# A fused Mamba-2 scan and mixture of experts on one core: how the decays of chunks 2 to 5 are made

## The chip, the core and the metric

The kernel runs on one core of a Trainium2 chip. Five engines work side by side, each through its own list of instructions in order: TensorE (PE in the profile; PEld is its weight load) multiplies matrices, VectorE (DVE) and GpSimd (POOL) work element by element, ScalarE (ACT) copies and applies functions such as the exponential, and SyncE (SP) issues most of the transfers (ScalarE issues a few). An engine that must wait for another waits on a semaphore, and everything behind that instruction in its list waits with it. TensorE writes its results to eight banks of an accumulation memory; a bank is free again when whoever reads it is done.

The metric is the device time of one execution in microseconds. The kernel before took 614.96 us, the median of three runs (614.61 to 615.97).

## The reference

Two parts follow each other. The first is a state-space scan (4 sequences, 8 heads, 768 steps, head width 32, state width 16). The reference takes the steps in chunks of 32; the kernel takes chunks of 128, which gives the same result. The second is a mixture of 4 experts on the 3072 tokens that come out, 256 wide, with 1024 hidden features in each expert.

```python
la = log(clip(a, 1e-6, 1));  cum = cumsum(la)            # within a chunk
L  = exp(cum[i] - cum[j]) * (i >= j)                     # the decays
y  = (C B^T * L) x + (C state) * exp(cum[i])
state = exp(cum[last]) * state + sum_j B_j x_j exp(cum[last] - cum[j])
...
p   = domain_probs / sum(domain_probs)
out = sum over experts e of p[:, e] * (relu(y @ w1[e]) @ w2[e])
```

L, the lower triangle of products of `a` between step j and step i, is what this case is about: each chunk of 128 steps and each head needs a square of 128 by 128 such decays.

## The kernel before

There are 24 chunks of 128 tokens; chunk c belongs to sequence c % 4, so chunks 0 to 3 are the first of their sequences and have no earlier state. Chunks go in pairs (two chunks share a token tile of 256 columns), and three pairs make a block; the experts' products on a block are done while the scan of the next block is under way.

**The experts.** `product` (L933) is the bulk of TensorE's work: two matmuls in the program of 128 by 128 weights against 256 columns, each shown as two records in the profile. For the first pair, chunks 0 and 1, the plain form is used: `plain_first(fb)` for four blocks fb of 256 hidden features, then the second layer. Everything after that uses sums and differences of weights and of tokens (a fast matrix product), made by DVE and POOL (L1024 for weights, L1043 for tokens, L960, L968, L1071 and others for the intermediate results). L968 applies the ReLU and the gate.

**The scan.** For a pair, `score` (L502) multiplies C by B on TensorE, four banks for the four quarters of the heads. The score is multiplied by the decays on DVE (L856), and `inner` (L546) multiplies the result with x and gives the outputs and the new state; `outputs` calls it for both chunks of a pair. `fade` (L540, POOL) makes the columns that lead to the state. `mask` (L495) makes the masked C.

**Three ways to the decays.** Chunks 0, 1 and 2: rows of `a` are loaded, clipped and set to zero at the first step, spread by TensorE over all partitions (`spread`, L660, ones against the rows, into four banks), and multiplied up by a scan on DVE (`scan`, L519, four of 256 columns for each chunk), which leaves the triangle L in the tile LT0. Chunks 3, 4 and 5 (`c < SCANNED`, 6): a transfer spreads the clipped rows over all partitions (`load_decays`, L463, 512 KB each, from the copy `acut_d`), and DVE scans two stretches of 512 columns. Chunks 6 and on: ScalarE takes the logarithm of `a`, DVE sums it along a chunk (L725), the sums go to `cum_d`; a transfer spreads a chunk's sums over the partitions, ScalarE makes exp(cum[i] - cum[j]) with -cum[j] as bias (`decay`, L526, one for each head), and POOL cuts the upper triangle away (`causal`, L531).

**The order.** Up to the first product the list is written out by hand: warm-up matmuls (`idle`, L684), chunks 0 and 1, the gates. The gates of the first block: the probabilities come by ScalarE's first DMA (L570), POOL and DVE turn them into shares (L614 to L619, with DVE's reciprocal in L618), TensorE transposes them (L646) into `p_sb`, and spreads those of four chunks (`spread_gate`, L652). From there on a planner (`Plan`) orders the work: `line` fixes TensorE's order, each piece has a cost and a due time, and the other engines and SP take pieces by due time. The line of the first block before: spread of chunk 2, two product blocks, `bias` (L1360: transposes of the sums, for the exponentials' bias), scores of 2 and 3, two product blocks, a part of the second layer, outputs of 2 and 3, and so on with chunks 4 and 5.

Of the kernel before, what the change touches and what calls it, by code (L numbers as in the profile page):

```python
# [35 lines left out]
SCANNED = 6  # L36
SCORED, OWN, LEAD, LEFT = 5, 2, 5, 3
# [322 lines left out]
def kernel(  # L360
# [26 lines left out]
    SPREAD = 3  # L387
# [21 lines left out]
    acut_d = tc.dram_tile([NCH, NH, P], FP32, name="acut_d")  # L409
# [11 lines left out]
    def some(n, shape, name, pool=const):  # L421
# [19 lines left out]
        "dram": [None],  # L441
    }
# [18 lines left out]
    def load_decays(c, ab):  # L461
        src = acut_d if c < SCANNED else cum_d
        nc.sync.dma_start(  # L463
            out=ab, in_=src[real(c)].rearrange("h s -> (h s)").partition_broadcast(P))
# [28 lines left out]
    def mask(c, ctm, xb):  # L493
        for t in range(NT):
            nc.scalar.mul(ctm[:, t], xb[:, OCT:OCT + P], tmask[:, t:t + 1])  # L495
# [28 lines left out]
    def decay(c, MT, ab, neg, h):  # L524

        nc.scalar.activation(  # L526
            out=MT[:, place(c, h), 0:P], in_=ab[:, h * P:h * P + P], func=AF.Exp,
            bias=neg[:, h % NT, NQ * real(c) + h // NT:NQ * real(c) + h // NT + 1])

    def causal(MT, h, n):  # L530
        nc.gpsimd.affine_select(  # L531
            out=MT[:, h:h + n, 0:P], in_=MT[:, h:h + n, 0:P], compare_op=ALU.is_ge, fill=0.0,
            base=0, pattern=[[0, n], [1, P]], channel_multiplier=-1)

    def fade(c, MT, xb, LT):
        b = xb[:, OB:OB + HN].rearrange("p (h n) -> p h n", h=NH)
        n = NH // 2 if place(c, 0) else NH
        for h in range(0, NH, n):
            to = slice(place(c, h), place(c, h) + n)
            nc.gpsimd.tensor_mul(  # L540
                MT[:, to, P:], b[:, h:h + n], LT[:, to, P - 1:P].to_broadcast([P, n, N]))

# [8 lines left out]
    def keep_state(c, A, y):  # L551
# [8 lines left out]
    aq0 = homes["V"][-1][:, 0].rearrange("p (t s) -> p t s", t=NT)  # L560
    aq1 = homes["V"][-2].rearrange("p c (t s) -> p c t s", t=NT)
    a_q = [aq0, aq1[:, 0], aq1[:, 1]]
# [3 lines left out]
    a_sb = homes["cum"][0]  # L566
    a_cut = homes["V"][-4][:NCH * NH // 2, 0].rearrange("p (r s) -> p r s", r=2)
    nc.gpsimd.memset(aq0, 0.0)
    nc.vector.memset(aq1, 0.0)
    nc.scalar.dma_start(out=pr, in_=probs)  # L570
    a_rows = a.rearrange("(i k) (q t) s -> k q i (t s)", k=NC, t=NT)[0]
    nc.sync.dma_start(
        out=aq0.rearrange("(q r) t s -> q r (t s)", q=NQ)[:, 0], in_=a_rows[:, 0])
    nc.scalar.dma_start(
        out=aq1.rearrange("(q r) c t s -> q r c (t s)", q=NQ)[:, 0], in_=a_rows[:, 1:SPREAD])
    nc.scalar.preload_act_table_set("natural_log_exp_and_others")

    xb = homes["xb"]
    nc.sync.dma_start(out=xb[0][:, OBT:], in_=xbc[real(0)][:, OBT:])
    nc.sync.dma_start(  # L580
        out=a_sb, in_=a.rearrange("c h s -> (c h) s").rearrange("(p r) s -> p r s", r=2))
    nc.sync.dma_start(out=xb[1][:, OBT:], in_=xbc[real(1)][:, OBT:])
    for c in range(2):
        nc.sync.dma_start(out=xb[c][:, :OBT], in_=xbc[real(c)][:, :OBT])
    for fb in range(2):
        load_w1(fb, homes["W"][fb])
    load_tokens(2, xb[2])
# [5 lines left out]

    tmask = const.tile([P, NT], FP32)
    nc.vector.memset(tmask, 0.0)
    for q in range(NQ):
# [4 lines left out]
    nc.vector.memset(zeros, 0.0)  # L601
    own = const.tile([P, 1], FP32)
    nc.vector.reduce_sum(
        own.unsqueeze(2), ident[:, 0].rearrange("p (q r) -> p r q", r=32)[:, 0:1],
        axis=mybir.AxisListType.X)

# [3 lines left out]
    clip(nc.vector, aq0.rearrange("p t s -> p (t s)"), own)  # L610
    nc.vector.memset(aq0[:, :, 0:1], 0.0)
# [10 lines left out]
    clip(nc.vector, aq1.rearrange("p c t s -> p (c t s)"), own)  # L622
    nc.vector.memset(aq1[:, :, :, 0:1], 0.0)

    clip(nc.gpsimd, a_sb)
    nc.gpsimd.tensor_copy(a_cut, a_sb)
    nc.gpsimd.memset(a_cut[:, :, 0:1], 0.0)

    def store_decays(engine, d, sb):
        engine.dma_start(  # L630
            out=d.rearrange("c h s -> (c h) s").rearrange("(p r) s -> p r s", r=2), in_=sb)

    store_decays(nc.sync, acut_d, a_cut)
    load_tokens(3, xb[3])
    for fb in range(2, 4):
        load_w1(fb, homes["W"][fb])
    for fb in range(4):
        load_w2(fb, homes["W"][4 + fb])
    load_decays(3, homes["ab"][0])
# [9 lines left out]
    def spread_gate(bank, gate):  # L649
        g = bank.rearrange("p (c s) -> p c s", s=P)  # L650
        for c in range(4):
            nc.tensor.matmul(  # L652
                out=g[:, c], lhsT=ident[:rows, 0, c * E:c * E + 1].to_broadcast([rows, P]),
                rhs=p_sb, start=(c == 0), stop=True, skip_group_check=True)
        nc.scalar.copy(out=gate[:, :4], in_=g)

    def spread(c, banks):
        for q, b in enumerate(banks):
            k = slice(32 * q, 32 * q + 32)
            nc.tensor.matmul(  # L660
                out=b[:, :NT * P], lhsT=one[k].to_broadcast([32, P]),
                rhs=a_q[c][k].rearrange("p t s -> p (t s)"),
                start=True, stop=True, tile_position=(32 * q, 0))
# [44 lines left out]
    nc.scalar.activation(out=a_sb, in_=a_sb, func=AF.Ln)  # L708
    next_ = [BANK[4], BANK[0], BANK[1], BANK[6]]
    scan_quarters(1, LT[1], four, 0)  # L710
# [9 lines left out]
    spread_gate(BANK[5], homes["gate"][0])  # L720
    for r in (3, 1, 2):
        masked(1, r, MT[1], LT[1], next_[r], 0)
    sums = homes["cum"][1]
    for r in range(2):
        nc.vector.tensor_tensor_scan(  # L725
            out=sums[:, r], data0=a_sb[:, r], data1=zeros[:NCH * NH // 2], initial=0.0,
            op0=ALU.add, op1=ALU.add)
    store_decays(nc.sync, cum_d, sums)
    ys = []
    for t in range(NT):  # L730
        y = BANK[6 + t][:, :P + N]
        ys.append(y)
        inner(1, t, y, xb[1], MT[1], P + N, True)
        nc.scalar.copy(out=yT0[:, t, P:], in_=y[:, 0:P])
    for t, y in enumerate(ys):
        keep_state(1, A[1][:, t], y[:, P:])
    mask(2, ctm[0], xb[2])
    nc.sync.dma_start(out=p_d.rearrange("e c s -> c e s"), in_=p_sb)

# [5 lines left out]
    now = 13.2  # L745
# [24 lines left out]
    yT[0, 0] = plan.taken("V", NV - 3, now)  # L770
    aq = plan.taken("V", NV - 2, 0.0)
    plan.homes["V"][NV - 4].free = now + 3.0
    plan.homes["W"][NW - 1].free = now
    for c, i in ((2, 2), (3, 3)):
        st[c]["xb"] = plan.taken("xb", i, now)
    st[2]["ctm"] = plan.taken("ctm", 0, now)
    st[3]["ab"] = plan.taken("ab", 0, now + 2)
    for c in range(2):
        st[c]["A"] = plan.taken("A", c, now)
    g0 = gates[0, 0] = plan.taken("gate", 0, now)  # L780
    LTv = [plan.taken("V", i, now) for i in range(4)]
    cum, cd, neg = plan.taken("cum", 1, now), plan.taken("dram", 0, now + 3.0), value("neg")

    def fetch(c):
# [9 lines left out]
        if "ab" not in s and c >= SPREAD:  # L794
            s["ab"] = value("ab")
            dma(lambda e: load_decays(c, s["ab"].t), 1, 512, part=[s["ab"]],
                reads=[cd] if c >= SCANNED else [])

    def decays(c):
        s = st[c]  # L800
        j = c % 2
        if not j:
            s["MT"] = st[c + 1]["MT"] = value("MT")
            s["made"] = st[c + 1]["made"] = []
# [759 lines left out]
```

## Time and profile before

| What | Value |
|---|---|
| Median of three runs | 614.96 us (614.61 to 615.97) |
| The profiled execution | 617.03 us, its span 615.3 us |
| TensorE busy | 605.7 us, 98% of the span |
| DVE, ACT, POOL busy | 489.5, 292.5, 157.6 us |
| Moved by DMA | 99.65 MB, mean 162 GB/s |
| First product (L933) starts | 13.28 us |
| Scan of chunk 3 starts | 19.13 us |
| Outputs of chunks 2 and 3 | 24.98 to 27.19 us |

The span is the time from the first instruction to the last on the core; the execution's own time has 1.7 us more around it. Busy time of TensorE counts a matmul from its issue to a modelled end, so a slow or waiting stretch can hide in it: the waits and the granted clock say more. In the timeline each line has start, length, engine, source line, operation, output and input, shape, count, and in brackets the idle time before it with what ended it. Idle time of an engine that nobody waits for costs nothing.

### The profile page before, as it was taken

The numbers are of one execution on the slowest core, as the hardware profiler recorded it, in microseconds if no ns is written. First come the engines' busy times: TensorE is split into PE (matmuls) and PEld (weight loads), VectorE is DVE, ScalarE is ACT, GpSimd is POOL, SyncE is SP. The second block draws the span as 40 slices with busy tenths as digits, with TensorE's granted clock in tenths as the row PEclk, the third lists the DMA queues.
The fourth block names the chain that finished last, engine by engine and source line by source line (L and its number), as shares of the span: only waits on it lengthen the run. The fifth ranks groups of instructions, "written<-read, shape, count | busy, mean of one in ns | idle before, by whom it ended". The sixth has DMA issues, their size and how long they took to land.

```text
span 615.3 us, 10136 instructions
## 1 busy us (share of the span) xinstructions
PE 605.7 (98%) x3365; PEld 514.8 (84%) x3365; DVE 489.5 (80%) x854; ACT 292.5 (48%) x681; POOL 157.6 (26%) x238
## 2 busy tenths in 40 slices
PE   9899999999999999999999999999999999999997
PEld 5677878888888888888888888888888888888885
DVE  7879897998969895697978988386785979576775
ACT  4237646378651327877443333844444242434441
POOL 5536556636372000776500100210000000000000
PEclk9899999999999999999999999999999999999999
DMA  7737578676863429983442424964233232964001
GB/s 249 256 114 231 204 218 300 205 224 208 280 188 94 134 34 285 297 291 146 132 144 77 137 63 118 284 222 137 61 111 87 93 90 51 303 230 126 1 0 52
DMA packets 89060, 99.65 MB, mean 162 GB/s; under 512 B 27428, under 2 KB 58928, under 8 KB 89008
## 3 DMA queue, kind: packets, MB, share of 16 engines
q1 hardware_dynamic: 88852, 98.95, 51.4%
q8 instruction: 27, 0.44, 0.3%
q14 instruction: 25, 0.20, 0.1%
q10 hardware_dynamic: 156, 0.06, 0.0%
HBM read 78.80 MB, written 20.17 MB: 161 GB/s over the span
## 4 chain that ended last, share of the span: by engine, by line
PE 92%; DVE 2%; ACT 1%; issue 0%; DVEq 0%
PE bank L933 88%; PE bank L546 2%; PE bank L502 1%; PE bank L879 1%; DVE v L960 1%; DVE v L968 1%; ACT A L556 1%; DVE MT L856 0%; ACT v L894 0%; DVE bank L1071 0%; DVE v L1260 0%; PE bank L1325 0%; DVE v L1425 0%; ACT LT L894 0%; ACT v L1330 0%
## 5 line engine op out<-in xcount | busy, mean ns | idle before, releaser
L933 PE MATMUL bank<-v,w 128*128 128x256 f32 x1716 | 402.0, 381 | 1.1 <-DVE bank L1071 0.8
L933 PEld LDWEIGHTS bank<-v,w 128*128 128x128 f32 x1716 | 325.7, 191 | 50.0 <-issue 2.9
L933 PE MATMUL bank<-Y,w 128*128 128x256 f32 x692 | 177.3, 381 | 0.7 <-ACT LT L894 0.4
L933 PEld LDWEIGHTS bank<-Y,w 128*128 128x128 f32 x692 | 130.2, 190 | 21.9 <-issue 1.7
L1213 ACT COPY v<-bank 128x512 f32<-128x512 f32 x109 | 63.9, 586 | 177.5 <-PE bank L933 165.2
L968 DVE SCALAR_TENSOR_TENSOR v<-bank,gate 128x512 f32<-128x512 f32 x147 | 101.0, 688 | 39.6 <-PE bank L933 36.8
L960 DVE TENSOR_TENSOR v<-v,v 128x512 f32<-128x512 f32 x179 | 125.9, 720 | 2.1 <-ACT v L942 0.8
L1024 POOL TENSOR_TENSOR w<-w,w 128x256 f32<-128x256 f32 x94 | 72.1, 784 | 46.0 <-DVE v L960 13.8
L1071 DVE TENSOR_TENSOR bank<-bank,v 128x512 f32<-128x512 f32 x81 | 55.5, 696 | 35.2 <-PE bank L933 23.6
L942 ACT COPY v<-bank 128x512 f32<-128x512 f32 x97 | 56.7, 587 | 55.0 <-PE bank L933 46.7
L947 ACT COPY bank<-v 128x512 f32<-128x512 f32 x126 | 73.2, 594 | 10.8 <-DVE v L968 8.7
L526 ACT ACTIVATE MT<-ab,neg 128x128 f32<-128x128 f32 x144 | 46.9, 393 | 2.0 <-DMA ab<-cum_d 2.0
L933 PE MATMUL bank<-LT,w 128*128 128x256 f32 x168 | 42.6, 380 | 0.0
L531 POOL TENSOR_SCALAR_AFFINE_SELECT MT<-MT 128x512 f32<-128x512 f32 x36 | 23.0, 652 | 67.8 <-ACT MT L526 53.9
L933 PEld LDWEIGHTS bank<-LT,w 128*128 128x128 f32 x168 | 31.8, 190 | 4.6 <-DVE v L968 0.3
L1024 POOL TENSOR_TENSOR w<-w 128x256 f32<-128x256 f32 x32 | 24.2, 762 | 23.2 <-DVE Y L1043 9.0
L960 DVE TENSOR_TENSOR v<-bank,v 128x512 f32<-128x512 f32 x26 | 17.9, 689 | 11.7 <-PE bank L933 9.9
L1260 DVE TENSOR_TENSOR v<-v,v 128x256 f32<-128x256 f32 x58 | 22.9, 431 | 1.1 <-ACT v L1213 0.7
L856 DVE TENSOR_TENSOR MT<-bank,MT 128x512 f32<-128x512 f32 x36 | 22.7, 681 | 0.1
L968 DVE SCALAR_TENSOR_TENSOR v<-v,gate 128x512 f32<-128x512 f32 x26 | 19.7, 758 | 0.4
L1213 ACT COPY LT<-bank 128x512 f32<-128x512 f32 x12 | 7.0, 586 | 23.5 <-PE bank L933 23.5
L840 POOL TENSOR_TENSOR cts<-ctm,dec 128x256 f32<-128x256 f32 x20 | 14.5, 734 | 11.6 <-DVE v L960 5.1
(110 smaller groups left out, 322.1 us busy)
## 6 DMA issues: line engine op xcount, KB each, us to landing
w<-w_d SPq DMA_DIRECT2D x128, 256.0 KB
w_d<-w SPq DMA_DIRECT2D x64, 256.0 KB
w<-in_w_dram SPq DMA_DIRECT2D x40, 256.0 KB
ab<-cum_d SPq DMA_DIRECT2D x18, 512.0 KB
w<-in_w_dram SPq DMA_DIRECT2D x64, 128.0 KB
gate<-p_d SPq DMA_DIRECT2D x15, 384.0 KB
xb<-in_xbc_dram SPq DMA_DIRECT2D x17, 192.0 KB
out_dram<-v SPq DMA_DIRECT2D x144, 16.0 KB
```

Source lines behind the costliest of these rows:

```text
L526: nc.scalar.activation(out=MT[:, place(c, h), 0:P], in_=ab[:, h * P:h * P + P], func=AF.Exp, bias=neg[:, h % NT, NQ * real(c) + h // NT:NQ ...
L531: nc.gpsimd.affine_select(out=MT[:, h:h + n, 0:P], in_=MT[:, h:h + n, 0:P], compare_op=ALU.is_ge, fill=0.0, base=0, pattern=[[0, n], [1, P ...
L856: nc.vector.tensor_mul(to, g, LT0[:, js, h] if cs[0] < SCANNED else to)
L933: nc.tensor.matmul(out=o, lhsT=w[:, j], rhs=x if half is None else x[:, j], start=(start and j == 0), stop=(j == 1), skip_group_check=True)
L942: act(.5, lambda e: nc.scalar.copy(out=flat(v), in_=bank.t), reads=[bank], writes=[v])
L947: act(.54 if to - lo > FB else .32, lambda e: nc.scalar.copy(out=bank.t[:, lo:to], in_=flat(v)[:, lo:to]), reads=[v], writes=[bank])
L960: plan.add(engines, lambda e: (on(e).tensor_add if sign > 0 else on(e).tensor_sub)(flat(v), whole(x), whole(y)), reads=[x, y], writes=[v], ...
L968: dve(D512, lambda e: nc.vector.scalar_tensor_tensor(out=h.t, in0=whole(x).rearrange("p (j m) -> p j m", j=JJ), scalar=0.0, in1=g.t[:, 2 * ...
L1024: plan.add(B256, lambda e, r=r, x=x, y=y, sign=sign: (on(e).tensor_add if sign > 0 else on(e).tensor_sub)(view(r), view(x), view(y)), two= ...
L1071: dve(D512, lambda e: (nc.vector.tensor_add if sign > 0 else nc.vector.tensor_sub)(to.t, bank.t, whole(x)), reads=[x, bank], writes=[to])
L1213: act(.5, lambda e: nc.scalar.copy(out=flat(v), in_=bank.t), reads=[bank], writes=[v], hold=HOLD)
L1260: plan.add(engines, lambda e: (on(e).tensor_add if sign > 0 else on(e).tensor_sub)(o[1](), x[1](), y[1]()), reads=[v for v in vs if v is n ...
```

## The change

Chunks 2 and 3 (the third and fourth) and chunks 4 and 5 no longer use DVE's scan.

The logarithms are made earlier: `a` as a whole is ScalarE's first DMA, DVE clips it, ScalarE takes the logarithm, DVE sums it, ScalarE stores the sums to `cum_d`; two small transfers on SP fetch rows of the sums (`log` for chunks 2 and 3, `log45` for 4 and 5).

Chunks 2 and 3: `lay` puts cum[i] - cum[j] into four banks on TensorE: a matmul spreads the row over the partitions, and matmuls with the rows as weights and minus one as the other operand subtract it down the columns. `grow` lets ScalarE make the exponential of two heads at once. Both stand in the part written by hand, around the outputs of chunk 1; in the changed kernel `lay` is L555 and L561, `grow` L567. The upper triangle is cut away in the pieces of `cut`.

Chunks 4 and 5: `spread` puts the sums of both chunks into four banks, and ScalarE's `decay` reads them there, with the bias as for later chunks.

`causal` and `mask` get a form for DVE (L538, L496 of the changed kernel), and for chunks below `SHARED_CUTS` the planner may give a piece to either engine.

The gates: the probabilities come by SP's fourth DMA in place of ScalarE's first; `spread_gate` is gone, and the first block's gates are loaded from `p_d` by two transfers on SP, after ScalarE has stored them. The transposes for the bias move to the part written by hand. Three broadcasts of 512 KB and the copy `acut_d` are gone. On TensorE's line the pieces of chunks 2 to 5 are put in by place, `BEFORE = (2, 4, 6, 10, 16)`: scores of 2 and 3 before the third half block of products, the spread of 4 and 5 before the fifth, outputs of 2 and 3 before the seventh, scores of 4 and 5 before the eleventh, outputs of 4 and 5 before the seventeenth. The planner starts from other times.

```diff
-SCANNED = 6
-SCORED, OWN, LEAD, LEFT = 5, 2, 5, 3
+FIRST_CHUNKS = 6
+SHARED_CUTS = 6
+BEFORE = (2, 4, 6, 10, 16)
+SCORED, LEAD = 5, 5
...
+    def lay(c, banks):
+        j = c % 2
+        to = [b.rearrange("p (c t s) -> p c t s", c=2, t=NT)[:, j] for b in banks]
+        for q in range(NQ):
+            k = slice(32 * q, 32 * q + 32)
+            nc.tensor.matmul(
+                out=to[q], lhsT=own[k].to_broadcast([32, P]), rhs=log[k, j], start=(j == 0),
+                stop=False, tile_position=(32 * q, 0), skip_group_check=True)
+        for t in range(NT):
+            for q in range(NQ):
+                k = slice(32 * q, 32 * q + 32)
+                nc.tensor.matmul(
+                    out=to[q][:, t], lhsT=log[k, j, t], rhs=less[k].to_broadcast([32, P]),
+                    start=False, stop=True, tile_position=(32 * q, 0), skip_group_check=True)
+
+    def grow(MT, r, bank, j):
+
+        nc.scalar.activation(
+            out=MT[:, j, NT * r:NT * r + NT, 0:P],
+            in_=bank.rearrange("p (c t s) -> p c t s", c=2, t=NT)[:, j], func=AF.Exp)
...
-    nc.scalar.dma_start(out=pr, in_=probs)
...
     nc.scalar.dma_start(
-        out=aq1.rearrange("(q r) c t s -> q r c (t s)", q=NQ)[:, 0], in_=a_rows[:, 1:SPREAD])
+        out=a_sb, in_=a.rearrange("c h s -> (c h) s").rearrange("(p r) s -> p r s", r=2))
     nc.scalar.preload_act_table_set("natural_log_exp_and_others")
+    nc.gpsimd.memset(aq, 0.0)
+    nc.sync.dma_start(**rows_to(aq, by_rows(a, 0)[:, 0:2]))
...
+    for c in range(2):
+        nc.sync.dma_start(out=xb[c][:, OBT:], in_=xbc[real(c)][:, OBT:])
+    nc.sync.dma_start(out=pr, in_=probs)
...
+    nc.vector.memset(log, 0.0)
+    nc.vector.memset(log45, 0.0)
...
+    clip(nc.vector, a_sb)
+    clip(nc.vector, aq.rearrange("p c t s -> p (c t s)"), own)
+    nc.vector.memset(aq[:, :, :, 0:1], 0.0)
+    nc.scalar.activation(out=a_sb, in_=a_sb, func=AF.Ln)
...
+    for r in range(2):
+        nc.vector.tensor_tensor_scan(
+            out=sums[:, r], data0=a_sb[:, r], data1=zeros[:NCH * NH // 2], initial=0.0,
+            op0=ALU.add, op1=ALU.add)
+    store_rows(nc.scalar, cum_d, sums)
+    nc.sync.dma_start(**rows_to(log, by_rows(cum_d, 0)[:, 2:4]))
+    nc.sync.dma_start(**rows_to(log45, by_rows(cum_d, 1)[:, 0:2]))
...
-    spread_gate(BANK[5], homes["gate"][0])
+    lay(2, four)
+    for r in range(NQ):
+        grow(grown, r, four[r], slice(0, 1))
     for r in (3, 1, 2):
         masked(1, r, MT[1], LT[1], next_[r], 0)
...
     for t in range(NT):
+        inner(1, t, y[:, t], xb[1], MT[1], P + N, t == 0)
+    nc.vector.tensor_copy(yT0[:, :, P:], y[:, :, 0:P])
+    lay(3, four)
+    for r in range(NQ):
+        grow(grown, r, four[r], slice(1, 2))
+    keep_state(1, A[1], y[:, :, P:])
...
+    bs = st[4]["a"] = st[5]["a"] = [value("bank") for _ in range(NQ)]
+
+    def both(e):
+        for c in (4, 5):
+            spread(c, [b.t for b in bs], log_.t.rearrange("p c (t s) -> p c t s", t=NT), c % 2 * NT * P)
+
+    visits.append(lined(lambda: pe(1.1, both, reads=[log_], writes=bs)))
+    for c in (4, 5):
+        decays(c)
+    visits.append(lined(outputs, [2, 3]))
...
+    for x, w in enumerate(fill):
+        for y, v in zip(BEFORE, visits):
+            if x == y:
+                line.extend(v)
+        line.append(w)
```

## The prediction

> **What bounds the kernel now.** I read the page first (busy shares, the clock by slices), then TensorE's waits, then a table of stretches, then the timeline of the first 28 us.
>
> ```profile
> PE 605.7 (98%) x3365; PEld 514.8 (84%) x3365; DVE 489.5 (80%) x854; ACT 292.5 (48%) x681; POOL 157.6 (26%) x238
> ...
> PEclk9899999999999999999999999999999999999999
> ...
> PE 92%; DVE 2%; ACT 1%; issue 0%; DVEq 0%
> ```
>
> TensorE is busy 98% of the span and carries 92% of the chain that ended last. No product is added or removed, so the time can move only by when the products begin, by idle TensorE, or by its clock.
>
> ```profile
> PE bank L546 <- POOL w L1024: 1.4, 1, 1.4
> PE bank L933 <- DVE bank L1071: 0.8, 1, 0.8
> PE bank L546 <- DVE MT L856: 0.7, 1, 0.7
> ```
>
> TensorE's waits (us, times, longest). The largest and the third stand ahead of L546, the outputs of chunks 2 and 3.
>
> ```profile
> 20.00:25.00 5.00, 3.64 (x18) 2.90 (x17) 4.90 (x8) 1.95 (x6) 3.34 (x6) 1.00 0.67 210
> 25.00:30.00 5.00, 4.30 (x39) 3.25 (x40) 4.91 (x6) 2.16 (x10) 3.61 (x4) 0.74 0.79 270
> 30.00:35.00 5.00, 5.00 (x32) 3.69 (x32) 3.98 (x6) 0.81 (x2) 2.17 (x5) 0.92 0.04 15
> ```
>
> Stretches: length, then busy time and count of PE, PEld, DVE, ACT and POOL, granted clock, DMA share, GB/s. Straight after the wait the clock is 0.74 and 0.92: 5 x 0.26 + 5 x 0.08 = 1.7 us of TensorE lost. The timeline says why outputs 2 and 3 are late:
>
> ```profile
> 11.23 0.47 SPq L463 DMA_DIRECT2D ab<-acut_d  x1
> ...
> 18.17 5.45 PE L933 MATMUL bank<-v,w 128*128 128x256 f32 x24
> ...
> 19.13 1.23 DVE L519 TENSOR_TENSOR_SCAN LT<-ab,ident 128x512 f32<-128x512 f32 x1 [1.90 <-DMA ab<-acut_d]
> ...
> 20.85 1.39 DVE L519 TENSOR_TENSOR_SCAN LT<-ab,ident 128x512 f32<-128x512 f32 x1
> ...
> 26.08 1.18 PE L546 MATMUL bank<-MT,xb 128*32 128x144 f32 x30 [0.70 <-DVE MT L856]
> ...
> 27.19 3.19 PE L933 MATMUL bank<-v,w 128*128 128x256 f32 x7
> ```
>
> Chunk 3's broadcast of 512 KB is issued at 11.23 and read at 19.13; two scans and the products of L856 follow, and TensorE, done with its products at 18.17 + 5.45 = 23.62, starts the next at 27.19. Of these 3.57 us the outputs need 1.18; 2.4 are lost. A later cluster (stops at 50.75, 77.31 and 86.81, together some 2.2 us, DVE or ACT named) is not touched by the edit; I leave it as it is.
>
> **The change, part by part.**
>
> *Removed after the first product.* Chunk 3's load and scans: the 2.4 us stop goes, and with it the clock's 1.7. The two transposes of L1360 go ahead of the products: 16.83 to 17.09, 0.3. Ten scans leave DVE (four of 0.6, six of 1.2 to 1.4; some 10 us), and three broadcasts leave the queue. DVE is 21.2 us busy of 26.7 between 13.3 and 40, so what it gains is cover, not time.
>
> *Added there.* Chunks 4 and 5 are spread by TensorE: eight matmuls in the program, sixteen in the records, of the shape of chunks 2 and 3's scores, which run from 17.09 to 18.17: +1.1.
>
> *What is late next.* Count from the first product, T; four product records take 0.87 (the chain has 67.61 us for 312), and a block of the first layer is eight. Scores 2 and 3 at T+1.8 wait for nothing (ScalarE's exponentials of chunk 3 end by T+1.8). Cuts: three on POOL (0.65), one on DVE (0.76, as L968 from SBUF), the fade (0.41) by T+3. Then DVE makes four score products and two gated products, 0.62 apart: T+6.8. TensorE reaches outputs 2 and 3 after the second and third product blocks and the spread, at T+7.7: cover 0.9. For chunks 4 and 5, sixteen exponentials go at 0.30 apart (L526, nine in 2.72) with 2.8 us of copies and masks queued among them, T+6 to T+14; the last cut, the fade and four score products end at T+17.7; TensorE comes there at T+19: cover 1.3. Gate loads on SP wait for the store of the gates (from ScalarE at about 10.5) and land near 15.5, before the first gated product at about 20; behind them wait the fourth first-layer block and all second-layer weights, landing by 22, used from T+8.9 on: nothing.
>
> *Paid ahead of the first product.* Two terms.
>
> (1) The gates' load goes from ScalarE's first DMA to SP's fourth, and VectorE's reciprocal of the sums stands, in order, before the first scan.
>
> ```profile
> 0.81 0.39 ACTq L570 DMA_DIRECT2D pr<-in_probs_dram  x1
> ...
> 2.72 0.26 POOL L614 TENSOR_TENSOR pairs<-pr 128x48 f32<-128x48 f32 x1 [0.28 <-DMA pr<-in_probs_dram]
> ...
> 3.74 0.30 DVE L618 RECIPROCAL total_p<-total_p 128x24 f32<-128x24 f32 x1
> ...
> 5.35 2.43 DVE L519 TENSOR_TENSOR_SCAN LT<-bank,ident 128x256 f32<-128x256 f32 x4 [0.87 <-PE bank L660]
> ```
>
> SP now starts behind POOL's clearing of 512 columns (0.31 for 256, 0.20 for 128: 0.53, from 0.80 to 1.33). Its first issue took 0.72 with four rows, ScalarE's eight-row one 1.19; then two token loads, 0.39 and 0.43. The gates' issue is at 3.0 to 3.5; 1.9 later POOL starts, 1.3 later the reciprocal is done: 6.2 to 6.7, or 7.0 with 0.3 for the loads ahead. The scans, and all of VectorE's unbroken row from 5.35 to 11.97 behind them, are later by 0.9 to 1.7. It could be 0.1 if the load lands sooner than the row says. I take 0.9, by SP's own 0.72. The 0.97 us of two more clearings and the two sums of logarithms on VectorE end before that: nothing. ScalarE's store of the sums also waits in its queue (for the gates' semaphore) to about 5.3, its masks follow by 6.5, and the warm-up matmuls hold TensorE to 6.84 as before.
>
> (2) `lay(2)` and `lay(3)` stand on TensorE around chunk 1's outputs, and `lay(3)` waits, bank by bank, for `grow` of chunk 2. Let s be the shift of (1). The second scans free the last bank at 10.8+s (the sums' rows, behind some 2 MB of loads, land near 11). Then 0.3 for its spreading and 16 narrow matmuls: 0.53 (half of the scores' 1.06) to 0.85. Four exponentials of 256 columns: 0.39 for 128 columns plus 0.11 for 128 more (the copies of 256 and 512 columns, 0.37 and 0.59), 0.41 apart: 1.73 to the last. `lay(3)` again 0.3 and 0.53 to 0.85. T = 14.4 to 14.9 + s, against 13.28: 1.1 to 1.7. If banks are freed sooner, 0.5. I take 1.1: L546's 32 in 1.18, 0.037 each at 144 columns, is the nearest row.
>
> Sum: -2.4 - 1.7 - 0.3 + 1.1 + 0.9 + 1.1 = -1.3 us. The profiled execution's own time is 617.03 (span 615.3, 1.7 around it), 2.07 above the median of the three runs, 614.96. I take the sum off the median: 613.7.
>
> *The clock.* In this trace 2.1 us of waits with narrow matmuls between them were enough for 1.7 us of lost clock. The opening of the changed kernel has such gaps too: between chunk 0's spread and outputs, and in `lay(3)`, which waits 1.7 us for ScalarE. Before the first product this trace shows no drop.
>
> The Trainium skill, "TensorE: Matmul & The Clock Gate", section "What's actually happening", says that the clock falls to half after at least one idle window of some 3.4 us and that windows run freely. By that rule neither kernel's gaps would cost anything, and the sum would be +0.4 (no 1.7 to win); the row shows the loss behind a shorter stop, so the row decides, and the rule's result (no 1.7 won) is in the second rival.
>
> **The rivals.**
> - *The opening is hardly late*: the gates land early (0.1) and `lay(3)` costs 0.5. -2.4 - 1.7 - 0.3 + 1.1 + 0.6 = -2.7: 612.3; with the later stops shorter by 1, 611.3. For it: the 1.9 is that of the first DMA of all. Against: the reciprocal stands before the scans. 0.22.
> - *It doesn't pay*: s 1.7 and `lay` 1.7: -3.3 + 3.4 = +0.1, 615.1, or the 1.7 of clock is not won back: -1.3 + 1.7, 615.4. For it: both are within the rows. 0.18.
> - *Slower, the clock falls in the opening*: `lay(3)`'s wait and the long scans leave TensorE sparse, and 1.7 is lost again at the first products. It decides once s plus `lay` pass 2.8: 1.4 + 1.7 gives -0.2 + 1.7 = +1.5, 616.5. Against it: before, a nearly as sparse opening kept its clock. 0.13.
> - *The wait moves to chunks 4 and 5*: ScalarE's queue runs 2.8 us over its 8, the cover of 1.3 goes, 1.5 is lost: +0.2, 615.2, to 616.5 with late weights. 0.07.
>
> **How the numbers follow.** The forecast has 0.40: 613.7, its own range 612.9 to 614.5. A measurement of this kernel tells 0.2% (1.2 us) from no change. Faster than 613.7 by that bound: 0.24 of the forecast's 0.40 and the first rival's 0.22, 0.46. Same: 0.16 of the forecast, 0.14 of the second rival, 0.05 of the last, 0.35. Slower: the clock's 0.13, the second's tail 0.04, the last's 0.02, 0.19. The range 611.0 to 616.6 leaves out a tenth at each end.
>
> **What would show it.** Right: no wait before the outputs of chunks 2 and 3, granted clock 1.00 from 20 to 35, the first scan at 6.2 and the first product at 15.2 to 15.5, VectorE idle on POOL before the reciprocal. Wrong: the first product before 14.3 or after 16.5; a clock below 1 near it; a wait before chunk 4's outputs; later stops (50 to 90 us) that differ by over 1 us.

## The result and the profile after

The changed kernel takes 618.12 us (median of 22 runs, 616.4 to 619.89), the kernel before 615.2 us beside it (22 runs, 613.65 to 617.69). The ratio is 1.0041, 95% interval [1.003, 1.0051]: slower by 0.4%, where 613.7 was forecast. The profiled execution of the changed kernel took 618.09 us, its span is 616.4, so 1.7 us lie around the span as before.

The page after, the lines that answer to those of before (busy time of TensorE, granted clock by slices, the chain that ended last by engine):

```profile
PE 609.2 (99%) x3413; PEld 516.6 (84%) x3413; DVE 481.0 (78%) x844; ACT 295.7 (48%) x696; POOL 166.7 (27%) x251
...
PEclk8999999999999999999999999999999999999999
...
PE 96%; DVE 2%; ACT 1%; issue 1%; ACTq 0%; DVEq 0%
```

TensorE is as dense as before or denser, and yet its first slice of clock is below full. Its waits (us, times, longest), the largest three of the changed kernel:

```profile
PE bank L710 <- PEq L1588: 0.8, 1, 0.8
PE bank L1354 <- DVE v L1289: 0.7, 1, 0.7
PE bank L962 <- ACT LT L923: 0.4, 1, 0.4
```

No wait stands ahead of the outputs (L574 now, L546 before): the 1.4 and the 0.7 are gone. The stretches say where the clock went (length, busy time and count of PE, PEld, DVE, ACT and POOL, granted clock, DMA share, GB/s):

```profile
10.00:13.30 3.30, 2.95 (x27) 1.41 (x26) 3.10 (x7) 1.29 (x5) 0.00 (x0) 0.53 0.37 127
13.30:17.00 3.70, 3.48 (x48) 2.51 (x47) 0.26 (x2) 1.82 (x7) 2.34 (x4) 0.50 0.43 136
...
20.00:25.00 5.00, 5.00 (x45) 3.71 (x45) 3.76 (x7) 0.81 (x4) 4.78 (x9) 1.00 0.73 224
25.00:30.00 5.00, 5.00 (x51) 4.05 (x50) 2.18 (x6) 4.26 (x19) 3.17 (x5) 1.00 0.92 293
30.00:35.00 5.00, 5.00 (x35) 3.93 (x34) 3.73 (x9) 2.33 (x10) 2.82 (x5) 1.00 0.00 2
```

From 20 to 35 TensorE is never idle and its clock is 1.00, where before it had 3.64, 4.30 and 5.00 of 5 us at 1.00, 0.74 and 0.92. The price stands in the first two lines: before the first product the clock is at half. The trace's own records of the clock have it at 0.5 from 10.17 to 17.00 (two windows of 3.413 us); before, one such window began at 27.39.

The opening in the timeline (start, length, engine, line, operation, output and input, shape, count, idle time before it and what ended it), sorted by start:

```profile
5.61 0.27 POOL L666 TENSOR_TENSOR pairs<-pr 128x48 f32<-128x48 f32 x1 [2.30 <-DMA pr<-in_probs_dram]
...
6.57 0.30 DVE L670 RECIPROCAL total_p<-total_p 128x24 f32<-128x24 f32 x1 [1.94 <-POOL total_p L669]
6.79 2.37 DVE L520 TENSOR_TENSOR_SCAN LT<-bank,ident 128x256 f32<-128x256 f32 x4
...
11.19 1.36 ACTq L739 DMA_DIRECT2D p_d<-p_sb  x1
12.19 1.19 PE L574 MATMUL bank<-MT,xb 128*32 128x144 f32 x16
12.60 0.69 ACT L496 ACTIVATE ctm<-xb,tmask 128x128 f32<-128x128 f32 x2 [1.14 <-issue]
13.20 0.35 ACT L701 COPY w<-bank 128x256 f32<-128x256 f32 x1
...
13.60 1.24 PE L555 MATMUL bank<-v,own 32*128 32x256 f32 x8 [0.22 <-ACT w L701]
14.62 1.08 PE L561 MATMUL bank<-less,v 32*128 32x128 f32 x16
...
15.71 1.21 ACT L567 ACTIVATE MT<-bank 128x256 f32<-128x256 f32 x4 [1.80 <-PE bank L561]
...
18.04 1.99 PE L962 MATMUL bank<-v,w 128*128 128x256 f32 x8
```

Three things are to be seen. The gates' load holds POOL, POOL holds VectorE's reciprocal, and the first scan starts at 6.79 (before: 5.35). ScalarE's issue of the store of the gates (L739) keeps it for 1.36 us, the mask of chunk 2 follows, and only then the copy L701 that frees the bank on which `lay(2)` waits: 13.60. TensorE itself, at half its clock since 10.17, was done with the matmuls ahead of `lay(2)` (L574) at 12.19 + 1.19 = 13.38, and waits 0.22 for that copy. From `lay(2)` to the first product pass 4.44 us, 3.4 of them at half the clock. The first product is at 18.04, before it was at 13.28: +4.76.

What was bought with it: before, from the first product to the end of the span 615.3 - 13.28 = 602.0 us passed, now 616.4 - 18.04 = 598.4. So 3.6 were won behind the first product and 4.76 lost ahead of it, +1.1 between the two profiled executions. The medians differ by more, 2.9: the execution profiled before was one with a lost clock window, of which the kernel before has few and the changed kernel many. The mean granted clock, listed with each timed run, is 0.998 or more in 6 of the 22 runs of the changed kernel (median 616.68) and 0.991 to 0.994 in 16 (618.3).

### The profile page after: what moved, and what is told of

Its sections match the earlier page's. It is cut to its first block, busy times and chain, and to the rows that moved or that the text cites. A ratio compares the mean times of both kernels' runs of the same rounds, so it can differ in the third digit from the quotient of the medians.

```text
span 616.4 us, 10221 instructions
## 1 busy us (share of the span) xinstructions
PE 609.2 (99%) x3413; PEld 516.6 (84%) x3413; DVE 481.0 (78%) x844; ACT 295.7 (48%) x696; POOL 166.7 (27%) x251
## 4 chain that ended last, share of the span: by engine, by line
PE 96%; DVE 2%; ACT 1%; issue 1%; ACTq 0%; DVEq 0%
PE bank L962 89%; PE bank L574 2%; PE bank L503 2%; PE bank L710 1%; PE bank L686 1%; PE bank L908 1%; ACT A L584 1%; DVE v L989 1%; DVE v L997 1%; PE bank L555 0%; ACT v L923 0%; PE bank L561 0%; DVE bank L1100 0%; DVE v L1289 0%; ACTq L739 0%
## 5 line engine op out<-in xcount | busy, mean ns | idle before, releaser
L962 PE MATMUL bank<-v,w 128*128 128x256 f32 x1656 | 390.1, 380 | 0.6 <-DVE v L997 0.3
L962 PEld LDWEIGHTS bank<-v,w 128*128 128x128 f32 x1656 | 313.1, 190 | 47.5 <-issue 2.4
L989 DVE TENSOR_TENSOR v<-v,v 128x512 f32<-128x512 f32 x187 | 131.3, 721 | 2.4 <-ACT v L971 0.9
L1100 DVE TENSOR_TENSOR bank<-bank,v 128x512 f32<-128x512 f32 x88 | 59.9, 695 | 39.4 <-PE bank L962 26.1
L976 ACT COPY bank<-v 128x512 f32<-128x512 f32 (+1 forms) x126 | 73.0, 590 | 12.6 <-DVE v L997 10.3
L962 PE MATMUL bank<-LT,w 128*128 128x256 f32 x228 | 57.7, 379 | 0.0
L962 PEld LDWEIGHTS bank<-LT,w 128*128 128x128 f32 x228 | 43.2, 190 | 6.0 <-issue 0.2
L886 DVE TENSOR_TENSOR MT<-bank,MT 128x512 f32<-128x512 f32 x44 | 27.8, 679 | 2.5 <-POOL MT L547 1.3
L989 POOL TENSOR_TENSOR v<-v,v 128x512 f32<-128x512 f32 x5 | 6.4, 1279 | 50.3 <-DVE v L989 50.3
L997 DVE SCALAR_TENSOR_TENSOR LT<-bank,gate 128x512 f32<-128x512 f32 x21 | 14.4, 685 | 5.2 <-PE bank L962 4.7
```

What stands on the lines that cost most here:

```text
L886: nc.vector.tensor_mul(to, g, to)
L962: nc.tensor.matmul(out=o, lhsT=w[:, j], rhs=x if half is None else x[:, j], start=(start and j == 0), stop=(j == 1), skip_group_check=True)
L976: act(.54 if to - lo > FB else .32, lambda e: nc.scalar.copy(out=bank.t[:, lo:to], in_=flat(v)[:, lo:to]), reads=[v], writes=[bank])
L989: plan.add(engines, lambda e: (on(e).tensor_add if sign > 0 else on(e).tensor_sub)(flat(v), whole(x), whole(y)), reads=[x, y], writes=[v], ...
L997: dve(D512, lambda e: nc.vector.scalar_tensor_tensor(out=h.t, in0=whole(x).rearrange("p (j m) -> p j m", j=JJ), scalar=0.0, in1=g.t[:, 2 * ...
L1100: dve(D512, lambda e: (nc.vector.tensor_add if sign > 0 else nc.vector.tensor_sub)(to.t, bank.t, whole(x)), reads=[x, bank], writes=[to])
```

## The experiments

"T" is the start of the first product.

**The kernel before, once more.** No edit. Is the lost window of the profiled execution in the median?

> The kernel before, once more as a kernel of its own, so that each of its runs comes with its granted clock. Theory (the clock drop behind chunk 3's late outputs comes in some runs only, since the clock's windows run freely): the runs fall into two groups, those with a mean clock of 0.999 to 1.000 near 615.0 us and those with 0.996 to 0.997 near 617.0, about one in four in the second; then the 1.7 us that the prediction won back were not in the median to begin with. Rival (the drop is in every run): all runs at 0.996 to 0.997, one group, 615.2.

Measured: 615.66 (12 runs), 1.0012 [0.9999, 1.0026] against the same kernel beside it. The two groups are there: 7 runs at full clock with a median of 615.26, 5 at 0.996 to 0.997 with 617.28; of the 35 runs beside it 30 at 614.83 and 5 at 617.04. The profiled execution is one of full clock. Its waits and stretches:

```profile
PE bank L546 <- POOL w L1024: 2.1, 1, 2.1
...
PE bank L546 <- DVE MT L856: 0.7, 1, 0.7
```

```profile
20.00:25.00 5.00, 3.16 (x15) 2.44 (x13) 4.90 (x7) 1.93 (x6) 3.02 (x5) 1.00 0.60 191
25.00:30.00 5.00, 4.00 (x44) 3.23 (x44) 4.91 (x7) 2.15 (x10) 3.78 (x5) 1.00 0.86 296
30.00:35.00 5.00, 5.00 (x34) 3.52 (x32) 4.79 (x7) 2.18 (x4) 2.01 (x6) 1.00 0.03 9
```

The stop is there, longer than in the first trace (2.1 and 0.7), and the clock stays at 1.00. So the stop belongs to the kernel, the lost window only to some of its executions: the 1.7 us cannot be won from the median. The clock records suggest why. They change only at whole steps of 3.413 us, counted from 6.91 in the first trace and from 4.25 in this one. In the first, nearly the whole stop (23.62 to 27.19) lies in one step, 23.98 to 27.39; here a boundary at 24.73 cuts it (23.16 to 27.51) in two. Two traces fit this, they do not test it. Here T is 12.81 and 601.1 us follow (span 613.9).

**The gates by ScalarE again.** The changed kernel, with the gates' load taken off SP and put second on ScalarE: does s, the shift of the first scan, go back into T?

```diff
         out=a_sb, in_=a.rearrange("c h s -> (c h) s").rearrange("(p r) s -> p r s", r=2))
+    nc.scalar.dma_start(out=pr, in_=probs)
...
         nc.sync.dma_start(out=xb[c][:, OBT:], in_=xbc[real(c)][:, OBT:])
-    nc.sync.dma_start(out=pr, in_=probs)
```

> The changed kernel with the gates' load on ScalarE's queue, behind its first load, in place of SP's fourth. Theory (the reciprocal that waits for the gates holds VectorE's scans from 5.35 to 6.79, and everything up to the first product with them): first scan at 5.3 to 5.5, first product 1.4 earlier, at 16.6 where the clock drops and 15.4 where it does not; 616.7 or less against 618.1. Rival (what holds the first product is ScalarE's queue and the bank that it frees, not the scans): first scan earlier, first product still at 17.5 to 18, time within 0.5 of 618.1.

Measured: 617.26, 1.0033 [1.002, 1.0047]; 4 runs at full clock 615.85, 8 below it 617.9. The profiled execution (full clock, span 614.0) has the first scan at 5.45 in place of 6.79 and T at 15.60. Its opening:

```profile
9.70 1.34 ACTq L739 DMA_DIRECT2D p_d<-p_sb  x1
11.09 0.69 ACT L496 ACTIVATE ctm<-xb,tmask 128x128 f32<-128x128 f32 x2 [1.12 <-issue]
11.69 0.35 ACT L701 COPY w<-bank 128x256 f32<-128x256 f32 x1
...
12.09 0.71 PE L555 MATMUL bank<-v,own 32*128 32x256 f32 x8 [1.22 <-ACT w L701]
...
15.60 1.99 PE L962 MATMUL bank<-v,w 128*128 128x256 f32 x8
```

`lay(2)` comes 1.51 earlier, and TensorE now waits 1.22 for ScalarE: the second hold is shown, with its size at full clock. Not all of the 1.51 is s, for this execution also keeps its clock ahead of `lay(2)`. From `lay(2)` to T it takes 3.51 at full clock, against 4.44 at half. The theory's first product (15.4 without a drop) nearly came, its 616.7 did not: 8 of 12 runs still lose some clock.

**ScalarE's order.** The changed kernel, the store of the gates and the mask of chunk 2 put behind the copy that frees the bank.

```diff
-    nc.scalar.dma_start(out=p_d.rearrange("e c s -> c e s"), in_=p_sb)
-    mask(2, ctm[2], xb[2])
...
     aside(1, 0, next_[0])
+    nc.scalar.dma_start(out=p_d.rearrange("e c s -> c e s"), in_=p_sb)
+    mask(2, ctm[2], xb[2])
```

> The changed kernel with ScalarE's store of the gates (1.36 us of issue) and the mask of chunk 2 (0.7) moved behind the copy that frees the bank for lay(2). Theory (in runs with a full clock lay(2) waits for that copy, 13.20 to 13.55, about 1.2 longer than for TensorE's own work; in runs with the clock at half TensorE itself comes there only at 13.4): 0.2 less where the clock drops, 1.2 less where it does not: 618.0 and 615.5. Rival (the scans alone set the start): no change in either.

Measured: 616.65, 1.0028 [1.0013, 1.0043]; 4 at full clock 615.9, 8 below it 617.32. In the profiled execution the copy starts at 11.30 in place of 13.20, `lay(2)` at 12.20 with the first scan still late (6.48), and T is 16.60; the clock is at 0.5 from 11.52 to 14.93.

```profile
11.30 0.37 ACT L701 COPY w<-bank 128x256 f32<-128x256 f32 x1 [0.35 <-PE bank L503]
...
12.20 1.24 PE L555 MATMUL bank<-v,own 32*128 32x256 f32 x8
```

`lay(2)` is 1.4 earlier than in the changed kernel's trace, but here too the first scan (0.31 earlier) and the clock differ between the two traces. Between runs at full clock one edit is worth 0.8: 615.85 and 615.9 (four runs each), against 616.68 (six). The theory had 615.5 there.

**Both edits.** The diffs of the last two experiments together.

> Both edits. Theory (the opening is late by these two, and the clock drops because TensorE is left sparse by them): first scan at 5.4, lay(2) at 11.1, first product at 14.6 to 15.0, the clock at 1.00 from 7 us on in most runs; 614.6 to 615.2, level with the kernel before or just below it. Rival (the clock drops in the opening anyway, since lay and its waits leave TensorE sparse): first product at 15.8 to 16.5, clock 0.5 for 3.4 us or more, 616.0 to 616.7. Rival (the loss lies behind the first product, in the changed plan): 617 or more.

Measured: 616.1, 1.001 [0.9993, 1.0026]; 8 at full clock 615.72, 4 below it 617.77. T is 16.12, no earlier than with the first edit alone, because a third hold ends last (TensorE in the timeline):

```profile
12.65 0.71 PE L555 MATMUL bank<-v,own 32*128 32x256 f32 x8 [1.77 <-DMA v<-cum_d]
```

It waits for the rows of the sums. ScalarE issues their store at 4.80; SP issues the load of them at 10.67, 5.9 us later, and has issued the tokens of chunks 2 and 3 and the weight blocks 1 and 2 ahead of it (4.49 to 6.44). This execution has the longest such delay: with the same loads ahead it is 4.7 to 4.9 in the traces of the changed kernel, of its two single edits and of the filled opening, so the third hold is often shorter than here. The time is that of the first rival, but not for its reason: 8 of 12 runs keep the clock.

**The sums' load ahead of the others.** The kernel with both edits; SP issues the sums' load before the tokens of chunks 2 and 3 and the weight blocks 1 and 2.

```diff
-    for c in (2, 3):
-        load_tokens(c, xb[c])
-    for fb in range(1, 3):
-        load_w1(fb, homes["W"][fb])
...
     nc.sync.dma_start(**rows_to(log, by_rows(cum_d, 0)[:, 2:4]))
+    for c in (2, 3):
+        load_tokens(c, xb[c])
+    for fb in range(1, 3):
+        load_w1(fb, homes["W"][fb])
```

> Both edits of e3_both, and the transfer of the sums' rows for chunks 2 and 3 ahead of the loads of chunks 2 and 3's tokens and of two weight blocks. In e3_both the rows land at 12.6, since the store of the sums takes from 4.8 to past 10 with 1.2 MB of loads ahead on the same engines. Theory (that round trip through memory is the third thing that holds lay(2)): the rows' issue at 7 to 7.5, lay(2) at 11.0 to 11.2, first product at 14.4 to 14.7 against 16.1; 614.2 with a full clock. Rival (behind it the tokens or the weights are late and give it back): lay(2) at 11, but a wait for tokens or weights after it, first product or later time lost, 615.5 or more.

Measured: 615.24, 1.0007 [0.9995, 1.002], and all 12 runs at full clock. The store goes at 4.70, the load at 7.50: 2.8 where it was 4.7 to 5.9. TensorE in the timeline:

```profile
10.72 0.81 PE L555 MATMUL bank<-v,own 32*128 32x256 f32 x8
...
14.97 1.99 PE L962 MATMUL bank<-v,w 128*128 128x256 f32 x8
```

With the three holds gone T is 14.97, and the kernel is level with the one before. The theory had 14.4 to 14.7 and 614.2, so it was too hopeful: ScalarE's mask of chunk 2 now waits 1.10 for its tokens, and the exponentials behind it are late.

**A filled opening.** The changed kernel with more warm-up matmuls put in at three places (`idle`, results overwritten) where TensorE is sparse: does the clock fall because TensorE is sparse, and what does that cost?

```diff
     spread(1, four)
+    idle(BANK[0])
...
+    idle(BANK[1], 2)
     next_ = [BANK[4], BANK[0], BANK[1], BANK[6]]
...
+    idle(BANK[5])
     lay(2, four)
```

> The changed kernel with three extra matmuls into free banks in TensorE's gaps of the opening (512 columns behind chunk 1's spread, 256 behind the transposes, 512 ahead of lay(2)), some 2.1 us of work whose results are overwritten. Theory (the clock falls in most runs because TensorE is sparse from 7 to 13 us): a full clock in at least three runs of four in place of 6 of 22, median 616.7 to 617.2 against 618.1, the runs with a full clock unchanged or up to 0.4 later. Rival (the drop has another cause than TensorE's own work there): still about three runs of four with a clock of 0.993 to 0.994, 618.3 to 619.

Measured: 617.63 (6 runs, 617.54 to 618.07), 1.0044 [1.0029, 1.0059]; no run lost a window, where 16 of 22 did. The first two stretches of it, beside those of the changed kernel above (0.53 and 0.50):

```profile
10.00:13.30 3.30, 2.95 (x31) 1.46 (x30) 2.44 (x6) 1.17 (x4) 0.00 (x0) 1.00 0.37 123
13.30:17.00 3.70, 3.70 (x62) 2.67 (x62) 1.41 (x4) 1.95 (x8) 2.91 (x5) 1.00 0.45 129
```

So it is TensorE's sparse work that loses the clock; which of the three places counts was not taken apart. But T is 17.48 even so: ScalarE's list is untouched, with the copy at 13.32 (13.20 in the changed kernel), and the filler ahead of `lay(2)` holds TensorE to 13.97. The clock explains the step from 616.68 to 618.3 in the changed kernel, not the rest; the fillers themselves cost some 0.9 against the runs at 616.68.

**The kernel before, the broadcast earlier.** Chunk 3's broadcast is issued ahead of the weight blocks 2 and 3 and the second-layer weights: the stop alone is taken away, in the kernel before.

```diff
     store_decays(nc.sync, acut_d, a_cut)
     load_tokens(3, xb[3])
+    load_decays(3, homes["ab"][0])
     for fb in range(2, 4):
         load_w1(fb, homes["W"][fb])
     for fb in range(4):
         load_w2(fb, homes["W"][4 + fb])
-    load_decays(3, homes["ab"][0])
```

> The kernel before with one transfer moved: chunk 3's broadcast is issued ahead of the two first-layer and four second-layer weight loads, not behind them. Theory (the stop ahead of the outputs of chunks 2 and 3 comes from that load's late landing alone; the decays' engine does not matter): the scan of chunk 3 starts at 16.6 in place of 19.1, the outputs at 23.6, 2 us less lost there, and no clock drop behind it: 613.0 against 614.9. Rival (VectorE's scans themselves hold the outputs, whenever the load lands): the stop shrinks by less than 1, 614.2 or more. Rival (the weights that now stand behind it are late): a new wait of L933 for a weight before 24 us, 615 or more.

Measured: 616.08, 1.0023 [1.0008, 1.0038]; 7 at full clock 615.56, 5 below it 617.39, against 614.57 for 19 of the kernel beside it. The profiled execution (span 613.0, 614.78 us, the lowest of its 12) has the chunk 3 scan at 17.14, and the outputs wait only 0.4 (TensorE's waits):

```profile
PE bank L933 <- DVE v L968: 1.5, 2, 1.2
...
PE bank L546 <- DVE MT L856: 0.4, 1, 0.4
```

The 2.1 is gone and a wait of products on the gated products (1.2) is new: a later broadcast is awaited by VectorE's scan (1.42, at 29.79). This execution keeps 1.4 us of the stop (span less T: 599.7, against 601.1), the medians show none of it. Why the others of this kernel are slower than the one profiled stays open; the run does say that the stop's price cannot be read off by moving one load. Whether the kernel before could be rid of the stop in another way is therefore not settled.

**A shorter opening.** The version with the sums first; there the mask of chunk 2 (waiting for its tokens) and the store of the gates still stand ahead of `grow(2)` on ScalarE.

```diff
     turn_gates(BANK[7])
+    nc.sync.dma_start(out=p_d.rearrange("e c s -> c e s"), in_=p_sb)
...
     aside(1, 0, next_[0])
-    nc.scalar.dma_start(out=p_d.rearrange("e c s -> c e s"), in_=p_sb)
-    mask(2, ctm[2], xb[2])
...
     for r in range(NQ):
         grow(grown, r, four[r], slice(0, 1))
+    mask(2, ctm[2], xb[2])
```

> The version with both edits and the sums' early load has its first product at 14.97 us and a span of 613.3. There ScalarE reaches the four exponentials of chunk 2 at 12.63, 0.65 after the differences are laid (11.98), because the mask of chunk 2 (waiting 1.10 for its tokens) and the store of the gates stand ahead in its list. Here the mask stands behind those exponentials and SP issues the store of the gates. Theory (from the first product to the end of the span all versions with the change take 598.3 to 598.4, so the time is set by the first product alone): first product at 14.2 to 14.5, span 612.5 to 612.9, time 614.3 to 614.8, 0.4 to 0.9 below the version it is built on and at or just below the kernel before (ratio 0.998 to 1.000), granted clock 1.00 in the opening. Rival (what is pushed behind comes back later): the gates, the mask of chunk 2 or the weights behind the gates on SP land too late, the stretch from the first product to the end grows beyond 599, and the time stays at 615.2 or goes above it although the first product is earlier.

Measured: 615.43, 0.9999 [0.9982, 1.0017]. T is 14.23 as the theory had it, but 599.2 us follow (span 613.4): the rival is right about the rest. The masks of chunks 4 and 5 wait for their tokens, and the scores that need them take 1.80 in place of 1.15:

```profile
23.94 0.67 DVE L496 TENSOR_SCALAR ctm<-xb,tmask 128x128 f32<-128x128 f32 x2 [0.98 <-DMA xb<-in_xbc_dram]
...
26.93 1.80 PE L503 MATMUL bank<-ctm,xb 32*128 32x256 f32 x16
```

**The gates stored earlier on SP.** The same, with the store of the gates ahead of the weight blocks 1 and 2 and of the sums' load for chunks 4 and 5.

```diff
-    for fb in range(1, 3):
-        load_w1(fb, homes["W"][fb])
-    nc.sync.dma_start(**rows_to(log45, by_rows(cum_d, 1)[:, 0:2]))
...
     nc.sync.dma_start(out=p_d.rearrange("e c s -> c e s"), in_=p_sb)
+    for fb in range(1, 3):
+        load_w1(fb, homes["W"][fb])
+    nc.sync.dma_start(**rows_to(log45, by_rows(cum_d, 1)[:, 0:2]))
```

> In the version with the short opening the first product came at 14.23 us as expected, but its span of 613.4 leaves 599.2 behind it, not 598.4: the masks of chunks 4 and 5 waited for their tokens (0.98 and 0.99 at 23.94 and 24.65) and TensorE's scores of 4 and 5, from 26.93, came 0.65 longer. SP issues those token loads at 17.3 to 19.0, behind the gates' load at 14.83, which waits for the store of the gates issued at 11.04. Here SP issues the store of the gates ahead of the loads of the weight blocks 1 and 2, at about 9.3, so the gates' load at 13.0 to 13.6 and the token loads by 17.5. Theory (that wait is all that was given back): first product 14.1 to 14.4, scores of 4 and 5 without a wait, span minus first product 598.3 to 598.6, time 614.2 to 614.7, ratio 0.998 to 0.9995. Rival (every start earlier than about 15 us only moves the stop to the next load): the weight blocks 1 and 2, now 0.9 later, or the tokens of chunks 4 and 5 hold TensorE again by 0.5 or more, and the time stays at 615.2 to 615.5.

Measured: 614.35 (614.13 to 615.32), all 12 runs at full clock; the kernel before beside it 614.57; 0.9996 [0.9985, 1.0007]. In its timeline the gates' load on SP, the first product and the scores of chunks 4 and 5:

```profile
11.96 0.82 SPq L1399 DMA_DIRECT2D gate<-p_d  x2
...
14.30 1.99 PE L962 MATMUL bank<-v,w 128*128 128x256 f32 x8
...
26.99 1.15 PE L503 MATMUL bank<-ctm,xb 32*128 32x256 f32 x16
```

The scores are back to 1.15. This is the best version with the change: by the two ratios 0.45%, 2.8 us, below the change as it was given, and level with the kernel before within the interval.

The profiled executions side by side:

| Kernel | T | Span | Span less T |
|---|---|---|---|
| before, first trace (window lost at 27.39) | 13.28 | 615.3 | 602.0 |
| before, once more | 12.81 | 613.9 | 601.1 |
| before, the broadcast earlier | 13.28 | 613.0 | 599.7 |
| changed | 18.04 | 616.4 | 598.4 |
| gates by ScalarE | 15.60 | 614.0 | 598.4 |
| ScalarE's order | 16.60 | 614.9 | 598.3 |
| both | 16.12 | 614.5 | 598.4 |
| sums first | 14.97 | 613.3 | 598.3 |
| filled opening | 17.48 | 615.8 | 598.3 |
| shorter opening | 14.23 | 613.4 | 599.2 |
| gates stored earlier | 14.30 | 612.6 | 598.3 |

In these traces all versions with the change but one need 598.3 to 598.4 behind T, whatever happened ahead of it. For them the time is T + 598.35 + 1.7. Against a median of some 614.8 for the kernel before at full clock it pays for T below 14.75.

## Why the prediction was wrong

It gave 613.7 and a range up to 616.6; it was 618.1. The miss of 4.4 has two parts, and the formula just found divides it: with the predicted T of 15.28 (13.28 + 0.9 + 1.1) the kernel takes 615.3, not 613.7. So 1.6 of the miss lies in the step from the sum to the forecast, 2.8 in T. Two of the prediction's own signs of being wrong came: a first product after 16.5 and a clock below 1 near it.

**The 1.7 of clock, taken off the median: wrong.** The prediction read the drop behind the stop in the profiled execution, noted that this execution stood 2.07 above the median, and still took the sum off the median. The repeat shows the same stop, even longer, with no drop. The execution shown was one of the minority, and the drop was the larger part of its distance to the median; what the median does not hold cannot be won there. The second rival had "the 1.7 of clock is not won back: 615.4", which is what the formula gives for the predicted T. That 1.6 comes so near 1.7 is in part chance. Behind T 2.8 were won (601.1 against 598.35), and the sum without the clock had 1.6. Against that, the repeat has its own first product at 12.81, not 13.28, and its time, 615.66, stands 0.7 above the 614.96 from which the sum was taken.

**What the change does behind T: right.** The stop before the outputs of chunks 2 and 3 is gone, the spread costs its 1.15 (1.1 said), the transposes have moved. From T to the start of the 81st product record the kernel before needs 26.95 us (in the repeat), the versions with the change, but for the shorter opening, 24.68: 2.3 won, where -2.4 - 0.3 + 1.1 = -1.6 was worked out. By the prediction's reckoning the repeat's stop is 3.2 (products done at 23.16, the next at 27.51, 1.18 of work between) and not 2.4, which is the difference. Another 0.5 came from the later stop near 77 us, which the prediction left as it is (TensorE busy from 75 to 80: 4.20 before, 4.74 after).

**The covers: right.** Outputs 2 and 3 come at T+7.9 (said T+7.7), the last score product of VectorE ends 1.05 before (0.9). Outputs of 4 and 5 start at 37.86, the score products end at 36.90: 0.96, where 1.3 was said. The wait did not move to chunks 4 and 5. The gates and weights behind the store on SP cost nothing at the T that this kernel has; with T at 14.23 that cover was gone and 0.8 was lost (the shorter opening).

**Term (1), s = 0.9: too small here, within its range.** The order of things was as said (gates, POOL, reciprocal, scan), with the first scan at 6.79: 1.44. SP issued at 3.07, the earliest time given, but POOL started 2.5 later, not 1.9. It lay inside 0.9 to 1.7, and the low value was taken by the length of one issue. It also differs between executions: with the gates still on SP, POOL starts 2.2 after the issue in the trace of ScalarE's order and 2.0 in the filled opening, where the first scan is at 6.48 and 6.22. Against the 5.35 of before, s was 1.44, 1.13 and 0.87, and the 0.5 by which it missed belongs to one execution.

**Term (2), the bank is free at 10.8 + s: wrong.** That counted VectorE's scans as the last to free a bank. The last was ScalarE's copy L701, behind an issue of 1.36 and a mask of 0.69: `lay(2)` at 13.60 in place of 11.7. The prediction had counted the store of the gates as something that others wait for, not as work that holds ScalarE. At full clock this hold is a wait of 1.22 (the gates by ScalarE), and taking it away saves 0.8 of the time. In the profiled execution TensorE at half clock came nearly as late by itself (13.38), so there the two causes cover each other. The sums' rows, put near 11, land at 12.65 in the trace of both edits, where the other holds are gone; behind those holds that did not show. From `lay(2)` to T 3.5 pass at full clock, where 3.6 stood; the prediction's own parts add up to 3.4 to 4.0 (so 14.2 to 14.8 + s, not 14.4 to 14.9).

**The clock: the right rival, the wrong chance and size.** The fall in the opening had 0.13, with the remark that a nearly as sparse opening kept its clock. It took two windows in the profiled execution and stretched the serial chain of `lay` and `grow` by 0.9; it comes in 16 of 22 runs (the versions with one of the first two holds gone lose some clock in 8 of 12, with both gone in 4 of 12, with all three gone in none). The point from which it was to decide, s plus `lay` past 2.8, was passed by far (4.76, or 3.8 without what the clock itself added). The filled opening, with no window lost in six runs, shows that it is the sparseness that does it. That the drop depends on the execution was not considered for either kernel.

The sum of T in the profiled execution: s +0.5, ScalarE's list together with TensorE's half clock ahead of `lay(2)` +1.4, the half clock behind it +0.9, together the 2.8.

## What to carry to other kernels

Ask of the profiled execution where it stands among the runs before counting a loss in it as one that can be won: a lost clock window that is in one execution of five (20 of 104 here) is not in the median. Where work is moved into a hand-written opening, follow every engine's list up to the instruction that frees the bank, the issue of a transfer included, and give each its length; the last of three releasers showed only when the other two were gone. And before moving a stop elsewhere, work out the break-even in the place it goes to: here some 2.8 us were won behind the first product at full clock, and 4.76 were paid ahead of it.

## What the runs showed of the hardware

- The clock falls without any long idle stretch. In the window from 6.76 to 10.17, ahead of the fall in the changed kernel, no two matmul starts are more than 0.33 us apart; there are 17, all but one of 32 rows by 256 columns. In the version with the gates by ScalarE, a stretch of 1.5 us between two starts inside the window from 10.24 to 13.65 cost nothing, and with both edits one of 2.05 inside the window from 10.33 to 13.75 cost nothing either. The Trainium skill, "TensorE: Matmul & The Clock Gate", section "What's actually happening", says that the half clock comes after at least one idle window of some 3.4 us and that windows run freely, apart from the kernel's start. The length is what the records show (3.413), and a drop in only some executions fits windows that run freely; the idle window does not agree with these traces. What the threshold is, the runs don't say.
- The way from a store on ScalarE's queue to the load of the same rows on SP took 4.8 us (5.62 to 10.45, changed kernel; 4.7 to 5.9 over five traces) with the tokens of chunks 2 and 3 and two weight blocks issued ahead, and 2.8 (4.70 to 7.50; 2.8 to 3.1 over three) without them. The Trainium skill, "DMA: Bandwidth & Descriptors", section "Latency and other measured facts", says that memory latency grows under load and that a transfer's fixed cost is smaller when the load is lighter; the direction agrees.
- One issue of the store of the gates, 96 rows into [e, c, s] order, keeps ScalarE for 1.33 to 1.36 us in five traces and 1.66 in a sixth (both edits); issued by SP it takes 0.81 to 0.85 in the traces of three kernels.
